# Accumulating transfers, early matmuls and a new inverse order in a gated mixer on one core

## The chip, the cores and the metric

The kernel runs on one core of one Trainium2 chip. The metric is the device time of one execution in microseconds (us), median of three. The core has a matrix engine (PE, whose weight loads are listed as PEld), a vector engine (DVE), a scalar engine (ACT), GpSimd (POOL) and a queue engine (SP). Each works through its own list of instructions in order; they meet through semaphores. Sixteen DMA engines serve the transfers that SP, ACT and POOL issue.

## The reference

All tensors are bf16 with 2048 rows and 640 columns, batch 1. The long convolution runs along the rows, one filter a column.

```python
def reference(A_q, A_k, A_v, A_shift_k, A_ssm_k, A_ssm_D, B_x, B_w1, B_w2, B_w3, B_w4, gate_w):
    x = A_q
    g = _sigmoid((x * gate_w).sum(-1, keepdims=True))
    a = _A_ref(x, A_k, A_v, A_shift_k, A_ssm_k, A_ssm_D)
    b = _B_ref(x, B_w1, B_w2, B_w3, B_w4)
    return g * a + (1 - g) * b

# _A_ref: a short and a long convolution
k_shift = sum over t in 0..3 of (k delayed by 3 - t rows) * shift_k[:, 3 - t]
kv = k_shift * v
y = causal convolution of kv with ssm_k (2048 taps a column, by FFT) + kv * ssm_D
return q * y

# _B_ref: a two-layer mixer
h = gelu(layernorm(x) @ w1)                    # 640 -> 640
hs = (the four column groups of h shifted by 1, -1, 2, -2 rows) @ w2
x1 = x + hs
return x1 + gelu(layernorm(x1) @ w3) @ w4      # 640 -> 1536 -> 640
```

## The kernel before, in words

Everything lives in one SBUF tensor, `arena`, 128 partitions wide, and one PSUM tensor, `PS`. A row t is held as block c (0 or 1), partition p and offset rho (0 to 7): t = 1024 c + 8 p + rho. So a "row tile" is one (c, rho), 128 x 640. PSUM is used as four pairs of banks; a job on PE takes a pair, and ACT empties it.

The mixer. For each rho, batch statistics on DVE (L756, L758) give mean and variance, POOL takes the inverse root as a power (L750), `normal` writes a normalized tile into one of four XN buffers (on DVE, L595), PE transposes it (L788), ACT evicts, the first product (L822) follows, ACT applies gelu (L621), and for the fifth column tile POOL issues small shifting transfers (L862, tag "tail"). The second product (L926) is added to x held in PSUM (L905); ACT evicts x1 with a row sum and squares it with another (L607). Four groups g of two rho each go through the second norm (`sum_group`, `normal`), a DMA transpose on SP (L945), the third product (L965, gelu on ACT) and the fourth (L983, after a seed of x1 that ACT writes into PSUM, L909).

The convolution. The taps are transposed (L729, evicted at L735). kv is built on DVE for each (c, h), four blocks: two multiplications of 5120 elements a partition into TA and TB (two taps each), their sum (5120), a sum of the halves (2560) and the product with v (2560). A transform of 2048 points is split into two column halves (half 0, 1) and two classes of frequencies (kap 0, 1): `forward` does its matrix part (L1014) for taps ("h") and kv ("k"). Then DVE runs four product units in the order (0,0), (0,1), (1,0), (1,1): `butterfly` on both, `window` on kv, `pointwise` (complex products) and `fold`. All units use slots s0 and s1 as temporaries. `inverse` (L1137) follows for half 0 after the second unit and for half 1 after the fourth: eight tiles of 8 matmuls, two ACT evictions each scaled by the gate, then on DVE a product with q and a sum into X (tag "fin"), and transfers out on SP (L1156).

The order on each engine is not that of the code. The class `Prog` records nodes with their reads, writes and an estimated cost, and `_forward` simulates the engines, taking next what can start first and, among equals, what the table `PRIO` puts higher (by tag and stage). Its result is the program's order. Waits follow from the recorded reads and writes. `add_dma`, a transfer on POOL that adds its source to its target, exists in the kernel before, but the lists `KV_DMA` and `PW_DMA` that choose it are empty. `WARM` is 40: a single job of matmuls on a tensor of ones at the start, whose result nobody reads.

Of the kernel before, what the change touches and what calls it, by code (L numbers as in the profile page):

```python
# [31 lines left out]
class Node:  # L32
    __slots__ = ("idx", "eng", "fns", "deps", "users", "cost", "bytes", "kind", "job", "prio", "first", "seed",
                 "start", "end", "base", "ordinal", "seq", "waits", "inc", "value", "sem", "final", "snap", "missing",
                 "tag", "soft")

    def __init__(self, idx, eng, fns, cost, kind, tag):
        self.idx = idx
        self.eng = eng
        self.fns = fns  # L40
        self.cost = cost
        self.kind = kind
        self.tag = tag
        self.deps = set()
        self.users = []
        self.bytes = 0
        self.job = None
# [12 lines left out]
        self.missing = 0  # L60
        self.soft = ()

# [24 lines left out]
class Prog:  # L87
# [69 lines left out]
    def pe(self, fns, r=(), cols=0, tag="", job=None, bits=(True, True)):  # L157
# [3 lines left out]
        node = self._new("pe", fns, cost, "c", r, (), None, tag)  # L161
        node.first = not job.nodes
# [6 lines left out]
    def dma(self, queue, fn, r=(), w=(), nbytes=0, cost=0.4, kind="dma", group=None, final=False, tag=""):  # L169
        node = self._new(queue, [fn], cost, kind, r, w, group, tag)  # L170
        node.bytes = nbytes
        node.final = final
        return node
# [18 lines left out]
    RATE = 405e3  # L192

    def _forward(self):
# [8 lines left out]
        free = {e: 0.0 for e in ENGS}  # L203
# [5 lines left out]
        link = 0.0  # L209
        xlink = 0.0  # L210
        alink = 0.0
        LAT = self.LAT
# [16 lines left out]
        while left:  # L229
# [41 lines left out]
            free[e] = t + n.cost  # L271
            if n.kind == "c":
                n.end = t + n.cost
            elif n.kind == "dma":
                link = max(link, t + 0.8) + n.bytes / self.RATE
                n.end = link + (1.1 if n.final else 1.7)
# [3 lines left out]
            else:  # L280
                xlink = max(xlink, t + 1.0) + 1.2
# [115 lines left out]
def _bf16_bits(a):  # L397
# [5 lines left out]
WARM = 40  # L403
KV_DMA = []
PW_DMA = []
# [3 lines left out]
INV = (0, 1, 2, 3, 4, 5, 6, 7)  # L409
SEED2 = []  # L410
SEED4 = (0, 1, 2, 3, 4, 5, 6, 7)
PRIO = {
# [67 lines left out]
def bass_gated_mix__ssm_conv_h3__mixer_s_mlp__prompt_kernel(  # L480
# [42 lines left out]
    oST = alloc(11 * 128)  # L523
# [38 lines left out]
    MV1, VAR1, RS1, MV2, S1, S2, MEAN2, TMP2, VAR2, RS2 = [stat(i) for i in range(10)]  # L562
# [17 lines left out]
    def c_ts(n):  # L580
        return 0.07 + n / 3700.0

    def c_act(n, aps=0, acc=False, psum=True):
        return (0.05 if psum else 0.09) + n * 0.000833 + 0.1 * aps + (0.16 if acc else 0.0)
# [92 lines left out]
    for c in range(5):  # L677
# [7 lines left out]
    P.pe([(lambda e, ps: e.matmul(bank(ps, 0, 128), ones, ones, start=True, stop=True)) for _ in range(WARM)], r=[ones],  # L685
         cols=128 * WARM * 2, tag="warmpe", bits=(False, None))
# [92 lines left out]
    def normal(rho, c, mean, rs):  # L779
# [15 lines left out]
    for rhos in LN1_GROUPS:  # L795
        P.stage = rhos[0]
        bn_group(MV1, VAR1, RS1, rhos)
        for rho in rhos:
# [35 lines left out]
    for sc in range(4):  # L834
# [10 lines left out]
        for j, d0 in enumerate(SHIFT):  # L845
# [4 lines left out]
            for carry, lst in todo.items():  # L850
# [9 lines left out]
                else:  # L860
                    i = i.rearrange("p (r q) -> p r q", r=n)
                P.dma("pool", lambda e, ps, o=o, i=i: e.dma_start(o, i), r=[i], w=[o], nbytes=32 * 512 * n,  # L862
                      cost=0.55, group="tail", tag="tail")
# [47 lines left out]
    for g in range(4):  # L911
# [27 lines left out]
        else:  # L939
            sum_group(rhos)  # L940
        for rho in rhos:
            for c in range(2):
                b = normal(rho, c, MV2[:, rho, 2 * c:2 * c + 1] if g in LN2_DVE else MEAN2[:, rho, c:c + 1], RS2)
# [182 lines left out]
    def inverse(half, slot0, slot1, Qh):  # L1126
        P.stage = half
        Qs = [cplx(s).rearrange("p (r i b) d -> p r i b d", r=4, i=2) for s in (slot0, slot1)]
        for rho in INV:
# [12 lines left out]
            gb = XN[gy_i[0] % 4]  # L1142
            gy_i[0] += 1
            for c in range(2):
# [3 lines left out]
            g2 = gb.rearrange("p (c d) -> p c d", c=2)  # L1148
            hs = slice(320 * half, 320 * half + 320)
            tt(g2, g2, Qh[:, :, rho, :], ALU.mult, 640, tag="fin")  # L1150
            tt(X[:, :, rho, hs], X[:, :, rho, hs], g2, ALU.add, 640, tag="fin")
            if rho % 2 == 1:
                for c in range(2):
                    src = X[:, c, rho - 1:rho + 1, hs]
                    dst = rows(out, c)[:, rho - 1:rho + 1, hs]
                    P.dma("sp", lambda e, ps, src=src, dst=dst: e.dma_start(dst, src), r=[src], nbytes=128 * 1280,  # L1156
                          final=True, tag="out")
# [48 lines left out]
```

## Time and profile before

| what | value |
|---|---|
| median of three runs | 243.61 us (243.39 to 244.1) |
| profiled execution, its own time | 244.46 us |
| its span, first to last instruction | 242.4 us |
| busy: PE, DVE, ACT, POOL | 224.5, 221.8, 157.4, 32.8 us |
| mean granted clock of PE | 0.970 |
| bytes moved by DMA | 27.67 MB |
| products of two tiles on DVE (L590) | 184, 194.3 us |
| one-tile scalings on DVE (L595) | 47, 14.7 us |
| scalings and squares on ACT from SBUF (L607) | 18, 12.4 us |

Times inside the profile count from the start of the span. L12 is line 12 of the kernel. The line of a helper stands for all that records through it: L590 is every two-operand operation on DVE, L595 every scaling there, L621 every ACT eviction, L633 every load. PE's busy time comes from modelled ends, so a stretch that is called busy can hold waiting; counts of matmuls in a window tell more. Of a group "a | b, c | d <- e" a is the shape and count, b the busy us, c the mean ns of one, d the idle us before it and e what ended it.

### The profile page before, as it was taken

What the parts mean: (1) busy time and instruction counts of PE and PEld (TensorE: products, weight loads), DVE (VectorE), ACT (ScalarE), POOL (GpSimd) and SP (SyncE); (2) the same over time, 40 slices, a digit from 0 to 9 for tenths busy, and PEclk for the clock granted to TensorE, in tenths of its full rate; (3) what the DMA queues carried; (4) which work ended last, traced back from release to release, by engine and by line L of the source; (5) the groups of instructions that cost most, each with busy time, mean ns of one, the idle gap of its engine ahead of it and who ended that gap; (6) DMA issues with size and microseconds to landing.
All of it is one profiled execution on the core that took longest, in us unless ns stands there. A gap on an engine that the chain in (4) does not pass through costs nothing.

```text
span 242.4 us, 3935 instructions
## 1 busy us (share of the span) xinstructions
PE 224.5 (93%) x1574; PEld 142.3 (59%) x1586; DVE 221.8 (92%) x290; ACT 157.4 (65%) x255; POOL 32.8 (14%) x38
## 2 busy tenths in 40 slices
PE   7279989999999999699999999999999999999991
PEld 6147654678754577454475655576444677577770
DVE  3998889999999899989999989789999999999484
ACT  2066685489999998968744668752554951564583
POOL 1323743340014002040005000000000000000000
PEclk9756999999999999999999999999999999999999
DMA  6999998010029910905000083200080541010055
GB/s 227 389 416 331 356 395 257 7 41 1 3 65 334 177 33 0 315 12 108 4 0 0 0 108 67 45 3 0 0 216 3 127 117 30 0 54 3 0 162 164
DMA packets 26483, 27.67 MB, mean 114 GB/s; under 512 B 12657, under 2 KB 22258, under 8 KB 26338
## 3 DMA queue, kind: packets, MB, share of 16 engines
q1 hardware_dynamic: 24674, 21.57, 31.3%
q0 software_dynamic: 1648, 5.54, 7.2%
q10 hardware_dynamic: 144, 0.33, 0.5%
q8 instruction: 12, 0.20, 0.4%
q14 instruction: 5, 0.04, 0.1%
HBM read 21.66 MB, written 2.62 MB: 100 GB/s over the span
## 4 chain that ended last, share of the span: by engine, by line
PE 66%; ACT 16%; DVE 11%; POOL 3%; DMA 2%; issue 1%; ACTq 0%; DVEq 0%
PE PS L983 22%; PE PS L965 21%; ACT arena L621 11%; PE PS L1137 7%; DVE arena L590 7%; PE PS L1014 6%; PE PS L926 4%; ACT arena L735 4%; POOL arena L750 3%; PE PS L822 2%; DVE arena L595 2%; DMA arena<-in_A_q_dram 2%; DVE arena L756 2%; PE PS L788 1%; ACT arena L607 1%
## 5 line engine op out<-in xcount | busy, mean ns | idle before, releaser
L590 DVE TENSOR_TENSOR arena<-arena 128x2560 bf16<-128x2560 bf16 (+4 forms) x184 | 194.3, 1110 | 8.6 <-ACT arena L621 6.6
L621 ACT ACTIVATE arena<-PS 128x640 bf16<-128x640 f32 (+3 forms) x132 | 97.7, 831 | 45.4 <-PE PS L965 20.7
L965 PE MATMUL PS<-arena 128*128 128x512 bf16 x232 | 51.7, 379 | 2.5 <-ACT arena L621 2.0
L983 PE MATMUL PS<-arena 128*128 128x320 bf16 x384 | 53.5, 299 | 0.0
L621 ACT ACTIVATE arena<-PS,arena 128x320 bf16<-128x320 f32 (+1 forms) x48 | 27.7, 622 | 33.2 <-PE PS L983 31.1
L983 PEld LDWEIGHTS PS<-arena 128*128 128x128 bf16 x384 | 37.5, 98 | 15.2 <-ACT PS L909 0.2
L965 PEld LDWEIGHTS PS<-arena 128*128 128x128 bf16 x240 | 23.3, 98 | 29.4 <-issue 2.4
L1014 PE MATMUL PS<-arena 128*128 128x320 bf16 x224 | 34.2, 300 | 0.7 <-ACT arena L621 0.5
L1014 PEld LDWEIGHTS PS<-arena 128*128 128x128 bf16 x224 | 19.5, 97 | 14.4 <-ACT arena L621 6.6
L822 PE MATMUL PS<-arena 128*128 128x512 bf16 (+1 forms) x121 | 24.7, 361 | 1.8 <-ACT arena L621 1.4
L926 PE MATMUL PS<-arena 128*128 128x320 bf16 x160 | 24.3, 299 | 0.0
L750 POOL TENSOR_TENSOR arena<-arena 128x4 f32<-128x4 f32 (+1 forms) x9 | 17.5, 1949 | 37.5 <-DVE arena L590 26.3
L822 PEld LDWEIGHTS PS<-arena 128*128 128x128 bf16 x125 | 12.8, 106 | 11.5 <-issue 1.7
L926 PEld LDWEIGHTS PS<-arena 128*128 128x128 bf16 x160 | 15.7, 98 | 6.1
L595 DVE TENSOR_SCALAR arena<-arena 128x640 bf16<-128x640 bf16 (+3 forms) x47 | 14.7, 355 | 4.3 <-POOL arena L750 3.3
L1137 PE MATMUL PS<-arena 128*128 128x320 bf16 x128 | 18.0, 299 | 0.0
L756 DVE BATCH_NORM_STATS2 arena<-arena 128x6 f32<-128x320 bf16 x32 | 13.4, 463 | 3.6 <-DMA arena<-in_A_q_dram 2.7
L1137 PEld LDWEIGHTS PS<-arena 128*128 128x128 bf16 x128 | 12.5, 98 | 5.2 <-issue 0.3
L788 PE MATMUL PS<-arena 128*128 128x128 bf16 x80 | 7.2, 253 | 6.3 <-DVE arena L595 6.3
L607 ACT ACTIVATE arena<-arena 128x640 bf16<-128x640 bf16 (+2 forms) x18 | 12.4, 694 | 0.2
L862 POOL DMA_DIRECT2D arena<-arena x18 | 9.7, 543 | 18.5 <-ACT arena L621 18.5
L909 ACT ACTIVATE PS<-arena 128x640 f32<-128x640 bf16 x16 | 11.0, 734 | 0.1
(33 smaller groups left out, 71.3 us busy)
## 6 DMA issues: line engine op xcount, KB each, us to landing
arena<-in_B_w_dram POOLq DMA_DIRECT2D x4, 960.0 KB, 7.9
arena<-in_A_v_dram SPq DMA_DIRECT2D x4, 640.0 KB, 12.1
arena<-in_A_k_dram SPq DMA_DIRECT2D x4, 640.0 KB, 11.3
arena<-in_A_ssm_k_dram SPq DMA_DIRECT2D x5, 512.0 KB, 19.0
arena<-in_A_q_dram SPq DMA_DIRECT2D x4, 640.0 KB, 4.8
out_dram<-arena SPq DMA_DIRECT2D x16, 160.0 KB, 2.0
arena<-in_A_q_dram SPq DMA_DIRECT2D x7, 320.0 KB, 7.2
arena<-cG POOLq DMA_DIRECT2D x1, 1024.0 KB, 5.2
```

Of the source, the lines that this page charges most:

```text
L590: return dve(lambda e: e.tensor_tensor(o, a, b, op), [a, b], [o], c_tt(n), tag=tag, **kw)
L595: return dve(lambda e: e.tensor_scalar(o, a, s1, s2, op0=op0, **kw2), [a] + sc, [o], c_ts(n), tag=tag, **kw)
L607: node = P.op("act", lambda e, ps: e.activation(o, i, func, **kw), r=r, w=[o], cost=c_act(n, naps, acc is not None, psum=False), tag=tag, ...
L621: node = P.op("act", lambda e, ps: e.activation(ov, inner(ps), func, **kw), r=r, w=[o], cost=c_act(n, len(r), acc is not None), job=job, t ...
L750: P.op("pool", lambda e, ps: e.tensor_tensor(r, v, hv, ALU.pow), r=[v, HALF], w=[r], cost=1.1, tag="ln")
L756: dve(lambda e, o=o, x=x: e.bn_stats(o, x), [x], [o], 0.393, tag="bn", group=("bn", id(mv), rho, c))
L822: fns.append(lambda e, ps, b=b, c=c, lhsT=lhsT: e.matmul(bank(ps, b, 256 * n), lhsT, XT[:, c, r0:r0 + n, :], start=(c == 0), stop=(c == 4)))
L926: fns.append(lambda e, ps, hh=hh, ft=ft, lhsT=lhsT: e.matmul(bank(ps, hh, 320), lhsT, w2v[:, ft, 320 * hh:320 * hh + 320], start=False, st ...
L965: fns.append(lambda e, ps, b=b, ft=ft, c=c, sc=sc: e.matmul(bank(ps, b, 512), w3v[:, c, 128 * ft:128 * ft + 128], XT[:, c, 2 * sc:2 * sc + ...
L983: fns.append(lambda e, ps, hh=hh, ft=ft, lhsT=lhsT: e.matmul(bank(ps, hh, 320), lhsT, w4v[:, ft, 320 * hh:320 * hh + 320], start=False, st ...
L1014: fns.append(lambda e, ps, w=w, b=b, rhs=rhs, st=(first and n == 0), en=(n == len(ss) - 1): e.matmul(bank(ps, b, 320), w, rhs, start=st, s ...
L1137: fns.append(lambda e, ps, kap=kap, ri=ri, c=c, r=r, s=s, n=n: e.matmul(bank(ps, c, 320), GM[:, kap, ri, r, s, :], Qs[kap][:, r, ri, c, :] ...
```

## The change

- `KV_DMA = [1]`: for block c = 1, both h, the sum of TA and TB (5120) is no longer a DVE instruction but two accumulating transfers on POOL, of half of the tile each.
- `PW_DMA = [1, 2]`: in the units (0,1) and (1,0) two of the ten operations of `pointwise` (2560 each) become an accumulating transfer each.
- The 40 matmuls on ones become 35 jobs of five, which the planner may put wherever PE is free.
- `LN1_ACT`, `LN2_ACT`: the normalization of rho 4 to 7 in the first norm and of groups 1 to 3 in the second moves from DVE to ACT (an Identity with scale and bias), and a small DVE product makes the bias.
- `INV = (0, 4, 2, 6, 1, 5, 3, 7)`: the order of the inverse's tiles. `FIN2 = (0,)`: in half 0 the closing product and sum take two tiles (rho and rho + 4) at once. Transfers out go by one rho with both blocks rather than by two rhos of one block; their number and size stay.
- The planner's estimates change (start times of the engines, transfer rates, a clock model for PE, costs of some operations), and `PRIO` is replaced, so the order of instructions changes on all engines.

```diff
-    RATE = 405e3
+    RATE = 400e3
+    WINDOW = 3.4133
+    PHASE = 2.4
...
-        free = {e: 0.0 for e in ENGS}
+        free = {"pe": 1.0, "act": 0.7, "dve": 0.8, "pool": 1.1, "sp": 0.7}
...
+            cost = n.cost
+            if n.array:
+                w = int((t - self.PHASE) // self.WINDOW)
+                while window < w:
+                    warm = duty > (0.42 if warm else 0.75) * self.WINDOW
+                    window += 1
+                    duty, carry = carry, 0.0
+                if not warm:
+                    cost += n.array
...
-                link = max(link, t + 0.8) + n.bytes / self.RATE
-                n.end = link + (1.1 if n.final else 1.7)
+                link = max(link, t + 1.2) + n.bytes / self.RATE
+                n.end = link + n.land
...
-                xlink = max(xlink, t + 1.0) + 1.2
+                xlink = max(xlink, t + 1.0, link) + 1.2
...
-WARM = 40
-KV_DMA = []
-PW_DMA = []
+FILL = 35
+KV_DMA = [1]
+PW_DMA = [1, 2]
...
-INV = (0, 1, 2, 3, 4, 5, 6, 7)
-SEED2 = []
+LN2_ACT = (1, 2, 3)
+LN1_ACT = [4, 5, 6, 7]
+INV = (0, 4, 2, 6, 1, 5, 3, 7)
+FIN2 = (0,)
+SEED2 = ()
...
     def c_ts(n):
-        return 0.07 + n / 3700.0
+        return 0.068 + n / 2220.0
...
-    P.pe([(lambda e, ps: e.matmul(bank(ps, 0, 128), ones, ones, start=True, stop=True)) for _ in range(WARM)], r=[ones],
-         cols=128 * WARM * 2, tag="warmpe", bits=(False, None))
+    for _ in range(FILL):
+        P.pe([(lambda e, ps: e.matmul(bank(ps, 0, 128), ones, ones, start=True, stop=True)) for _ in range(5)], r=[ones],
+             cols=128 * 5, tag="fill", bits=(False, None))
...
+    def minus(nb, mean, rs):
+        dve(lambda e: e.scalar_tensor_tensor(out=nb, in0=mean, scalar=-1.0, in1=rs, op0=ALU.mult, op1=ALU.mult),
+            [mean, rs], [nb], 0.15, tag="ln")
...
+        if nb is not None:
+            act(b, X[:, c, rho, :], ACTF.Identity, 640, scale=rs[:, rho, c:c + 1], bias=nb[:, rho, c:c + 1], tag="xn")
+            return b
...
-        bufs = [normal(rho, c, MV1[:, rho, 2 * c:2 * c + 1], RS1) for c in range(2)]
+        bufs = [normal(rho, c, MV1[:, rho, 2 * c:2 * c + 1], RS1, NB1 if rho in LN1_ACT else None) for c in range(2)]
...
+        if g in LN2_ACT:
+            minus(NB2[:, rsl, 0:2], mean[:, rsl, :], RS2[:, rsl, 0:2])
...
+            pair = rho // 4 == 1 and half in FIN2
+            if half in FIN2 and not pair:
+                continue
...
+            if pair:
+                g2 = V(oXN + 640 * (i - 1), 1280).rearrange("p (s c d) -> p c s d", s=2, c=2)
+                sel = slice(rho - 4, rho + 1, 4)
...
+            n = 1280 if pair else 640
+            tt(g2, g2, Qh[:, :, sel, :], ALU.mult, n, tag="fin")
+            tt(xs, xs, g2, ALU.add, n, tag="fin")
+            for r1 in range(sel.start, sel.stop, 4):
+                dst = out[0].rearrange("(c p r) d -> p c r d", c=2, r=8)[:, :, r1, hs]
+                src = X[:, :, r1, hs]
```

The transfer that the two lists choose is unchanged:

```python
def add_dma(o, i, nbytes, tag):
    return P.dma("pool", lambda e, ps: e.dma_start(o, i, accum_op=ALU.add, max_dma_last_dim=2560), r=[o, i], w=[o], nbytes=nbytes, cost=0.9,
                 kind="acc", tag=tag)
```

More of the change, by code (lines that the diff above doesn't have):

```diff
@@ L61, in __init__ @@
         self.soft = ()
+        self.array = 0.0
+        self.land = 2.2
 def _granules(ap):
@@ L167, in pe, with dma @@
         return job
-    def dma(self, queue, fn, r=(), w=(), nbytes=0, cost=0.4, kind="dma", group=None, final=False, tag=""):
+    def dma(self, queue, fn, r=(), w=(), nbytes=0, cost=0.4, kind="dma", group=None, final=False, tag="", land=None):
         node = self._new(queue, [fn], cost, kind, r, w, group, tag)
@@ L172, in dma @@
         node.final = final
+        node.land = land or (1.1 if final else 2.2)
         return node
@@ L211, in _forward @@
         alink = 0.0
+        warm = False
+        window = -1
+        duty = carry = 0.0
         LAT = self.LAT
@@ L270, in _forward @@
             n.start = t
-            free[e] = t + n.cost
+            cost = n.cost
[7 more added lines that the diff above has]
+                    cost += n.array
+                if n.tag != "shk":
+                    inside = min(cost, self.PHASE + (w + 1) * self.WINDOW - t)
+                    duty += inside
+                    carry += cost - inside
+            free[e] = t + cost
             if n.kind == "c":
-                n.end = t + n.cost
+                n.end = t + cost
             elif n.kind == "dma":
-                link = max(link, t + 0.8) + n.bytes / self.RATE
-                n.end = link + (1.1 if n.final else 1.7)
+                link = max(link, t + 1.2) + n.bytes / self.RATE
+                n.end = link + n.land
             elif n.kind == "acc":
@@ L560, in stat @@
         return V32(oST + f * 128, 64).rearrange("p (r i) -> p r i", r=8)
-    MV1, VAR1, RS1, MV2, S1, S2, MEAN2, TMP2, VAR2, RS2 = [stat(i) for i in range(10)]
+    MV1, VAR1, RS1, MV2, S1, S2, MEAN2, TMP2, VAR2, RS2, NB2, NB1 = [stat(i) for i in range(12)]
     def gcol(f):
@@ L1147, in inverse @@
                 evict(job, o, lambda ps, c=c: bank(ps, c, 320), ACTF.Copy, 320, scale=GG[:, gi:gi + 1], tag="gy")
-            g2 = gb.rearrange("p (c d) -> p c d", c=2)
+            pair = rho // 4 == 1 and half in FIN2
+            if half in FIN2 and not pair:
+                continue
             hs = slice(320 * half, 320 * half + 320)
[L1150 to L1157, printed above, removed]
+            if pair:
+                g2 = V(oXN + 640 * (i - 1), 1280).rearrange("p (s c d) -> p c s d", s=2, c=2)
+                sel = slice(rho - 4, rho + 1, 4)
+            else:
+                g2 = gb.rearrange("p (c s d) -> p c s d", c=2, s=1)
+                sel = slice(rho, rho + 1)
+            xs = X[:, :, sel, hs]
+            n = 1280 if pair else 640
[4 more added lines that the diff above has]
+                src = X[:, :, r1, hs]
+                P.dma("sp", lambda e, ps, src=src, dst=dst: e.dma_start(dst, src), r=[src], nbytes=128 * 1280,
+                      final=True, tag="out")
         P.stage = ""
```

21 lines of the change are left out of this document (14 added, 7 removed), and 45 rows, old and new, of the table PRIO.

## The prediction

> **What bounds the kernel now.** I read the page's summary first, then the chain in order of time, then the groups by form, the windows and the waits. The page (busy us, and 40 slices of 6.06 us each):
>
> ```profile
> span 242.4 us, 3935 instructions
> ...
> PE 224.5 (93%) x1574; PEld 142.3 (59%) x1586; DVE 221.8 (92%) x290; ACT 157.4 (65%) x255; POOL 32.8 (14%) x38
> ...
> PEclk9756999999999999999999999999999999999999
> ...
> PE 66%; ACT 16%; DVE 11%; POOL 3%; DMA 2%; issue 1%; ACTq 0%; DVEq 0%
> ```
>
> PE and DVE are both over 90% busy, and PE had about half its clock in slices 2 to 4. The windows show where PE's time goes to waste (columns: window, length, PE, PEld, DVE, ACT, POOL busy with counts, clock, DMA share, GB/s):
>
> ```profile
> 10.60:24.30 13.70, 12.14 (x78) 8.23 (x79) 12.28 (x44) 7.91 (x11) 4.14 (x8) 0.55 1.03 377
> 24.30:48.30 24.00, 22.60 (x220) 13.42 (x222) 22.16 (x19) 14.61 (x17) 10.72 (x10) 1.00 0.73 255
> 67.00:82.00 15.00, 14.39 (x96) 7.46 (x94) 14.86 (x18) 15.00 (x28) 3.55 (x4) 1.00 0.74 209
> 95.20:103.20 8.00, 6.00 (x45) 3.96 (x45) 8.00 (x8) 7.88 (x17) 1.75 (x2) 1.00 0.73 243
> ```
>
> The end of the chain (start, length, what) shows that PE runs into the last evictions without a break:
>
> ```profile
> 223.19 3.26 PE PS L983 x24
> 226.45 10.88 PE PS L1137 x80
> ...
> 237.42 0.53 ACT arena L621
> ...
> 238.92 0.49 DVE arena L590
> ```
>
> **PE's floor.** From stretches of the chain where matmuls follow each other at full clock: 320 columns take 0.136 us (24 in 3.26), 512 columns 0.2155 (10 in 2.16), 256 columns half of that, a transpose 0.0655 (40 in 2.62). The code issues 928 x 0.136 = 126.0, 315 x 0.2155 = 67.9, 50 x 0.1075 = 5.4, 160 transposes 10.5, the gate's 85 single columns 2.4, the tap broadcast's eight 1.1: 213.3 us, and none of it is touched. The first transpose starts at 10.6 and 5.1 us follow the last matmul (237.3 to 242.4). So PE loses 242.4 - 213.3 - 10.6 - 5.1 = 13.4 us in between: in 10.6 to 24.3 it does 40 transposes, 30 matmuls of 256 columns and the eight (6.95 us of work in 13.7: 6.75 lost); 24.3 to 48.3 about 1.2; 67 to 82 does 92 x 0.136 = 12.5 in 15.0 (2.5 lost; ACT is 15.00 busy, evicting 640 columns in 0.6 us for each 0.54 us of matmuls); 95.2 to 103.2 45 x 0.136 = 6.1 in 8.0 (1.9, ACT again); 1.05 elsewhere.
>
> **The DVE chain.** From 83 us until the last fold at 223.8 (209.24 + 14.56 in DVE's timeline) DVE has hardly a gap: the four product units follow each other because they share two temporaries. Its prices by form:
>
> ```profile
> L590 DVE TENSOR_TENSOR arena<-arena 128x2560 bf16<-128x2560 bf16 x70 | 100.5, 1483 | 0.3
> ...
> L590 DVE TENSOR_TENSOR arena<-arena 128x5120 bf16<-128x5120 bf16 x12 | 33.7, 2821 | 0.1
> ...
> L595 DVE TENSOR_SCALAR arena<-arena 128x640 bf16<-128x640 bf16 x32 | 12.4, 437 | 4.3 <-POOL arena L750 3.3 <-DMA arena<-arena 0.9
> L607 ACT ACTIVATE arena<-arena 128x640 bf16<-128x640 bf16 x16 | 12.0, 753 | 0.2
> ```
>
> **The change, part by part.** *Off DVE:* two kv additions of 5120 (2 x 2.82 = 5.64), four product sums of 2560 (4 x 1.483 = 5.93), 8 first and 12 second normalizations (20 x 0.437 = 8.74); the first half's final products go in pairs (16 x 0.489 = 7.82 becomes 8 x 0.818 = 6.54, saving 1.28); five bias products come in (0.2 each by the 0.23 row, 1.0). Sum: 20.6 us less.
>
> *On to ACT:* 20 x 0.753 = 15.1 us by the square's row, the nearest. Eight lie near 27 to 38, where ACT is 3.9 to 4.7 busy of each 6: free. Twelve (9 us) belong to the second norm; transposes on SP and the third product wait for ACT now instead of DVE. ACT is full from 54 to 102 (46.6 of 48 us), and after that idle for 2 us and more at a time between evictions, so they cost 0 (late) to 9 (early); I take 1, set off below.
>
> *The adds:* eight of 640 KB issued on POOL, 0.87 each (the weight loads there took 0.85 to 0.88). No row shows one. The nearest by size, the q loads of 640 KB, landed in 4.8; the v loads in the crowded start in 12.1. A small transfer between arena ranges landed in 1.8 when nothing else ran, so 4.8 is 1.8 plus 3.0 for bytes. An add also reads its target: I take half again, 4.5. In a unit the second add goes out two products (2.97) after the first and two more products cover it: it lands at 0.87 + 1.8 + 2 x 4.5 = 11.7, the products end at 5.9, DVE stalls 5.8. With 1 for kv, whose fourth-block products can run meanwhile: 2 x 5.8 + 1 = 12.6. Ends: 3.0 for bytes gives 2.7 a unit (6 in all, less if a window step fills in, so even nothing); the 12.1 row gives 10.3 for bytes, 17.3 a unit, 36 in all. Queued behind an add on POOL: the powers of the second norm and the w3, w4 and table loads, hence the third product; each waits at most for the products ahead of the add, and DVE's slack holds that.
>
> So the last fold ends at 223.8 - 20.6 + 12.6 = 215.8. After it PE needs 64 x 0.136 = 8.7 and the 5.1 of the end: a span of 229.6 by this chain, under PE's own figure below, so the stalls cost nothing. They decide beyond a sum of 16.4.
>
> *Early matmuls:* 175 in fives instead of 40. Forty took 4.45 us; 175 take 11.5 (0.0655 each) to 18.7 (0.107), so from 1.06 they reach past 10.6 and, in the gaps, beyond. A started five holds a real matmul up for 0.33 to 0.54, at most some eight times: 0 to 4, on PE time that waits for DVE anyway; I take 0. If the clock stays full, 6.95 us of work in 10.6 to 24.3 takes 6.95. But it helps only if DVE delivers: there it is 12.3 of 13.7 busy with the statistics, and 24 to 38 alternates kv products with normalizations behind a power of 3.5 us on POOL. Eight of those moving to ACT, the work up to the last of the first product (6.95 + 22.8 = 29.8) could end at 40.4 instead of 48.3. Of 7.95 lost I take back 6.5 (bounds: -4 and 7.95).
>
> *The rest:* the forward stretches keep the 0.6 against 0.54, but second-layer products, sooner ready, can lie between: 2.5 of 4.4 back, less 1 for ACT, net 1.5 (bounds -9, 4.4). Head: the first variance step stood 0.36 behind statistics of the next row, and the first transposes waited for both blocks: 0.5 (0 to 1.5). The last fold frees four of eight inverse tiles before its last two steps: today PE has other work until 226.45, 2.65 after the fold, so 0. Elsewhere 0.5 of 1.05. The output transfers keep count and size; the queue on SP gains none.
>
> Sum: 6.5 + 1.5 + 0.5 + 0.5 = 9.0. The profiled execution took 244.46 for its span of 242.4, 0.85 over the median of 243.61. It becomes 235.5 (span 233.4 = 10.1 + 213.3 + 4.9 lost + 5.1); from the median, **234.6**.
>
> **Rivals.**
> *ACT takes over.* If the twelve fall into 54 to 102, PE waits for evictions some 6 us more: 240.6. For: ACT 15.00 of 15. Against: in 108 to 150, where most of them lie now, ACT idles before evictions. 0.13.
>
> *Adds at half the rate.* Reading two operands where a load reads one would double the byte part to 6.0: 8.7 a unit, 18.5 in all, fold at 221.7, span 235.5: 236.7. The row is the 4.8 us load, and nothing here shows an add. The Trainium skill, "Collectives: The Full Stack", Part 3, says the adding transfer runs at half the copy's rate because it reads two sources; no run here shows that yet. 0.10.
>
> *DVE starves POOL's issue.* A power on POOL took 3.53 beside a 2.82 product and 0.71 to 1.04 without: if adds wait like that, 2.5 each, some 5 a unit and 2.5 for kv, 25.1 in all, fold at 228.3, span 242.1: 243.3. Against: four POOL transfers issued at 49.7 to 51.3 landed in 1.8 to 2.0 beside products without a gap. The Trainium skill, "SBUF — State Buffer", "SBUF: two separate sides", warns that a DMA from that queue stands while DVE holds the shared port; its later section excepts two-input products, as the 1.8 does. 0.04.
>
> *Nothing gained.* The clock drops again after the fills, or fills delay the transposes as much as they speed them: 243.5. 0.05.
>
> *Slower: the adds' bytes.* If one needs 9.6 us for its bytes (68 GB/s; the q load did 218), each middle unit stalls 16: 33 in all, fold at 236.2, span 250.0: 251.2. It is slower than now from a sum of 26, which is 7.9 us (83 GB/s) an add. For: the 12.1 row, and that no such transfer is in the trace. Against: from 100 us on the queues are nearly empty. 0.13.
>
> **Numbers.** Forecast 0.55, own range 228.5 (all 13.4 and 1.5 of the head back: 228.7) to 239. A measurement here tells 0.3%, 0.73 us, apart. Faster: 0.55 + 0.10 + 0.12 of ACT's 0.13 = 0.77. Within: 0.04 + 0.05 = 0.09. Slower: 0.13 + 0.01 = 0.14. The range 228.5 to 244.5 leaves out the slow case and little else.
>
> **What would show it.** Right: clock full from the second slice on, DVE near 201 busy, ACT near 172, the first product's last matmul before 43, DVE gaps of 3 to 9 ahead of the two subtractions of the middle units, PE unbroken to the last inverse. Wrong: a chain ending in DVE and DMA, gaps over 12 there, or PE waiting for ACT between 54 and 102.

## The result, and the profile after

The changed kernel takes 254.52 us (median of four runs, 250.85 to 256.79) against 243.50 us of the kernel before on the same chip (243.34 to 244.10): a ratio of 1.0365, 95% interval 1.0245 to 1.0485. It is slower by 9 to 11 us; forecast was 234.6, some 9 us faster. The ratio leaves out the two longest of the four runs, the profiled one among them, and so lies below the quotient of the medians (1.045); differences between this kernel and its variants are therefore given by medians and by ratios, and read from the traces as well. The profiled execution took 254.89 us for a span of 253.1.

The page after, in the lines that answer to those of before:

```profile
span 253.1 us, 4195 instructions
...
PE 233.6 (92%) x1711; PEld 149.2 (59%) x1721; DVE 202.8 (80%) x261; ACT 171.7 (68%) x275; POOL 38.6 (15%) x46
...
PEclk9999998999999999899999999999999999999899
...
DVE 45%; ACT 17%; DMA 15%; PE 9%; SPq 8%; issue 3%; POOL 1%; ACTq 0%; DVEq 0%; POOLq 0%
```

The early matmuls did hold the clock up, DVE did lose 19 us of work and ACT did gain 14. But the chain, which was 66% PE, is now 45% DVE and 15% DMA, with 9% PE. The chain in order of time (start, length, what) shows where:

```profile
21.96 14.46 DMA arena<-in_gate_w_dram
...
36.74 3.87 PE PS L859 x10
...
90.79 6.30 ACT arena L647 x12
...
98.08 1.57 DVE arena L616 x2
...
145.07 8.88 DMA arena<-arena
...
184.71 11.99 DMA arena<-arena
...
218.06 19.86 DVE arena L616 x16
...
238.06 10.54 PE PS L1178 x64
```

Four things are to be seen. The load of the gate's weights, issued behind all but one of the kv loads, lands 14.5 us later; PE, which stood 4.0 us for it, then runs ten matmuls of 512 in 3.87 us instead of 2.16, at a granted clock of 0.59 from 36.47 to 40.60. The first window step (98.08) starts when ACT has evicted the part of the kv transform that it reads (half 0, class 0); before, it started at 83.10. Two of the chain's pieces are accumulating transfers, the second sums of the two middle units (L655). And PE's last 64 matmuls start at 238.06, only when the third of the last fold's six steps has ended (237.91; the fold ends at 240.12). They take 10.54 us where 64 x 0.136 = 8.7 were counted: PE had stood for 3.6 us, and the granted clock was 0.52 from 238.06 to 241.50. (The Trainium skill, "TensorE: Matmul & The Clock Gate", Part 1, puts the idle time after which the clock falls at one window of some 3.4 us. The waits of 4.0 and 3.6 us agree; but the clock also fell after two waits of 2.8 us, to 0.64 from 106.01 to 109.50 here and to 0.53 in f_xn2 below, and it stood at 1.00 after one of 3.2 us in a_noadd. The length of a wait alone does not decide here.)

The windows (columns as in the prediction) show PE's front:

```profile
10.60:24.30 13.70, 13.65 (x147) 10.24 (x146) 12.39 (x43) 10.94 (x16) 7.26 (x12) 1.00 1.04 354
24.30:48.30 24.00, 19.07 (x118) 9.82 (x119) 19.70 (x13) 16.13 (x21) 6.13 (x6) 0.93 0.79 270
```

The clock column rose from 0.55 to 1.00 in the first, but in the second PE did 118 matmuls instead of 220. The waits of DVE (what it waited for: us in total, times, longest):

```profile
DVE arena L621 <- ACT arena L647: 13.5, 3, 6.7
DVE arena L616 <- DMA arena<-arena: 8.9, 2, 6.3
DVE arena L616 <- issue: 5.4, 1, 5.4
DVE arena L616 <- ACT arena L647: 5.4, 3, 3.5
```

The first row belongs to the front, the two between to the middle units. Of the last row 3.5 us are the wait ahead of the first window step, 1.0 comes at 180.05 and 1.0 behind the last fold. The lines of DVE's timeline for the window step, the first from the kernel before, and for the middle units (start, length, line, shape, count, idle before and what ended it):

```profile
83.10 7.55 DVE L590 TENSOR_TENSOR arena<-arena 128x1280 bf16<-128x1280 bf16 x8 [0.59 <-ACT arena L621]
...
98.08 20.24 DVE L616 TENSOR_TENSOR arena<-arena 128x1280 bf16<-128x1280 bf16 x18 [3.47 <-ACT arena L647]
...
154.03 25.02 DVE L616 TENSOR_TENSOR arena<-arena 128x2560 bf16<-128x2560 bf16 x24 [6.33 <-DMA arena<-arena]
...
191.25 2.96 DVE L616 TENSOR_TENSOR arena<-arena 128x1280 bf16<-128x1280 bf16 x3 [5.44 <-issue]
196.78 45.34 DVE L616 TENSOR_TENSOR arena<-arena 128x2560 bf16<-128x2560 bf16 x45 [2.56 <-DMA arena<-arena]
```

The time up to the last fold can be split at the first window step, with the gaps that DVE's timeline marks added up on both sides:

| | before | after |
|---|---|---|
| first window step starts | 83.10 | 98.08 |
| DVE idle ahead of it | 7.4 | 30.1 |
| from there to the end of the last fold | 140.7 | 142.0 |
| of that DVE idle | 4.5 | 15.3 |
| last fold ends | 223.80 | 240.12 |
| from there to the end of the span | 18.6 | 13.0 |

So DVE's work fell by 7.7 us ahead of the window step (83.10 - 7.4 against 98.08 - 30.1) and by 9.5 behind it (136.2 against 126.7). Ahead of it the saving became waiting and the step came 15 us later; behind it the waits ate the saving.

### The profile page after: what moved, and what is told of

Its sections match the earlier page's. It is cut to its first block, busy times and chain, and to the rows that moved or that the text cites. A ratio compares the mean times of both kernels' runs of the same rounds, so it can differ in the third digit from the quotient of the medians.

```text
span 253.1 us, 4195 instructions
## 1 busy us (share of the span) xinstructions
PE 233.6 (92%) x1711; PEld 149.2 (59%) x1721; DVE 202.8 (80%) x261; ACT 171.7 (68%) x275; POOL 38.6 (15%) x46
## 3 DMA queue, kind: packets, MB, share of 16 engines
q0 software_dynamic: 5360, 10.78, 20.6%
## 4 chain that ended last, share of the span: by engine, by line
DVE 45%; ACT 17%; DMA 15%; PE 9%; SPq 8%; issue 3%; POOL 1%; ACTq 0%; DVEq 0%; POOLq 0%
DVE arena L616 45%; ACT arena L647 11%; DMA arena<-arena 10%; SPq L659 8%; DMA arena<-in_gate_w_dram 6%; PE PS L1178 4%; PE PS L859 4%; ACT arena L762 4%; ACT arena L633 2%; POOL arena L899 1%; PE PS L963 1%; POOL arena L655 0%; PE PS L822 0%; PE PS L942 0%; ACTq L1227 0%
## 5 line engine op out<-in xcount | busy, mean ns | idle before, releaser
L616 DVE TENSOR_TENSOR arena<-arena 128x1280 bf16<-128x1280 bf16 (+5 forms) x170 | 181.6, 1126 | 25.3 <-DMA arena<-arena 8.9
L1006 PE MATMUL PS<-arena 128*128 128x512 bf16 x233 | 53.0, 385 | 3.2 <-ACT arena L633 2.8
L1024 PE MATMUL PS<-arena 128*128 128x320 bf16 x384 | 53.3, 299 | 0.0
L1024 PEld LDWEIGHTS PS<-arena 128*128 128x128 bf16 x384 | 37.5, 98 | 15.0 <-ACT PS L946 0.2
L1006 PEld LDWEIGHTS PS<-arena 128*128 128x128 bf16 x240 | 23.6, 99 | 30.9 <-issue 4.7
L1055 PE MATMUL PS<-arena 128*128 128x320 bf16 x224 | 34.7, 300 | 1.1 <-ACT arena L647 0.6
L633 ACT ACTIVATE arena<-arena 128x640 bf16<-128x640 bf16 (+2 forms) x38 | 30.3, 832 | 1.7 <-DVE arena L807 1.5
L1055 PEld LDWEIGHTS PS<-arena 128*128 128x128 bf16 x224 | 19.7, 98 | 15.1 <-ACT arena L647 7.4
L963 PE MATMUL PS<-arena 128*128 128x320 bf16 x160 | 24.3, 299 | 0.0
L1178 PE MATMUL PS<-arena 128*128 128x320 bf16 x128 | 19.7, 316 | 3.6 <-DVE arena L616 3.6
L655 POOL DMA_DIRECT2D arena<-arena x8 | 10.5, 1424 | 71.7 <-DVE arena L616 71.0
L621 DVE TENSOR_SCALAR arena<-arena 128x640 bf16<-128x640 bf16 (+3 forms) x27 | 6.9, 289 | 17.8 <-ACT arena L647 13.5
L777 POOL TENSOR_TENSOR arena<-arena 128x4 f32<-128x4 f32 (+1 forms) x9 | 13.8, 1531 | 41.5 <-DVE arena L616 29.2
L963 PEld LDWEIGHTS PS<-arena 128*128 128x128 bf16 x160 | 15.7, 98 | 6.1
L1178 PEld LDWEIGHTS PS<-arena 128*128 128x128 bf16 x128 | 13.1, 103 | 10.0 <-issue 4.2
L859 PEld LDWEIGHTS PS<-arena 128*128 128x128 bf16 x125 | 12.2, 101 | 11.1 <-issue 1.9
L783 DVE BATCH_NORM_STATS2 arena<-arena 128x6 f32<-128x320 bf16 x32 | 13.5, 463 | 2.6 <-DMA arena<-in_A_q_dram 2.6
L712 PE MATMUL PS<-arena 128*128 128x128 bf16 x175 | 12.7, 245 | 1.1 <-DVE arena L669 1.1
L712 PEld LDWEIGHTS PS<-arena 128*128 128x128 bf16 x175 | 12.2, 112 | 1.6 <-DVE arena L669 1.1
## 6 DMA issues: line engine op xcount, KB each, us to landing
arena<-in_A_ssm_k_dram SPq DMA_DIRECT2D x5, 512.0 KB, 11.7
```

What stands on the lines that cost most here:

```text
L616: return dve(lambda e: e.tensor_tensor(o, a, b, op), [a, b], [o], c_tt(n), tag=tag, **kw)
L633: node = P.op("act", lambda e, ps: e.activation(o, i, func, **kw), r=r, w=[o], cost=c_act(n, naps, acc is not None, psum=False), tag=tag, ...
L777: P.op("pool", lambda e, ps: e.tensor_tensor(r, v, hv, ALU.pow), r=[v, HALF], w=[r], cost=1.1, tag="ln")
L859: fns.append(lambda e, ps, b=b, c=c, lhsT=lhsT: e.matmul(bank(ps, b, 256 * n), lhsT, XT[:, c, r0:r0 + n, :], start=(c == 0), stop=(c == 4)))
L963: fns.append(lambda e, ps, hh=hh, ft=ft, lhsT=lhsT: e.matmul(bank(ps, hh, 320), lhsT, w2v[:, ft, 320 * hh:320 * hh + 320], start=False, st ...
L1006: fns.append(lambda e, ps, b=b, ft=ft, c=c, sc=sc: e.matmul(bank(ps, b, 512), w3v[:, c, 128 * ft:128 * ft + 128], XT[:, c, 2 * sc:2 * sc + ...
```

## The experiments

In all of these kernels but the last two, the order of every engine is written out, not planned: it is that of the kernel named as the base, with the moves that are told. They run on several chips, so each is compared with the kernel before on its own chip (243.96, 244.30, 244.28 and 244.44 us). A helper's line number differs from kernel to kernel: L723, L724 and L754 below are the same two-operand DVE operations as L616. Medians from two chips can differ by up to 0.9 us for that reason alone (243.50 against 244.44 for the kernel before); the ratios do not have this.

**One part at a time, on the kernel before.** First the kv sums (b_kva), with the third block's transfers behind the tail's on POOL and the fourth's behind a table load (one power moves up with them, ahead of a weight load):

```diff
-KV_DMA = []
+KV_DMA = [1]
```

> The kernel before in its own order, with only the two kv sums of block c = 1 made by four accumulating transfers. Theory A (kv's transfers cost because the next block's products write the same two temporaries): the next block's first product waits until both transfers have landed, some 9 us after the last product, where the sum took 2.8; twice, so the last kv step ends 10 to 14 us later, the first window step too, and the time is 253 to 258. Rival B (the transfers are hidden, ACT's 15 us of extra work made the change slower): 241 to 245. Rival C (the late loads of k and of the gate's weights made it slower): 241 to 245.

Measured: 263.69 us, ratio 1.081 (1.078 to 1.085). DVE's timeline (start, length, line, shape, count, idle before):

```profile
67.86 4.69 DVE L724 TENSOR_TENSOR arena<-arena 128x5120 bf16<-128x5120 bf16 x4 [8.59 <-DMA arena<-arena]
...
90.67 3.09 DVE L724 TENSOR_TENSOR arena<-arena 128x2560 bf16<-128x2560 bf16 x2 [13.31 <-DMA arena<-arena]
```

Both column halves of a block use the same TA and TB. So the fourth block's first product (67.86) waits 8.6 us until the third block's sums have landed, and the sum of its own halves (90.67) waits another 13.3 for its own transfers: 21.9 us of waiting for 5.6 us of work taken off. The prediction let the fourth block's products run meanwhile.

The same with temporaries of its own for the fourth block (b_kvabuf), in XT (the transposed rows of the first norm), its products right behind the third's, and its transfers ahead of the table load:

```diff
-    for c in range(2):
-        TA = V(oTAP if c == 0 else oS, 5120)
-        for h in range(2):
+    kv_block(1, 0, V(oS, 5120), TB)
...
+    kv_block(1, 1, V(oXT, 5120), V(oXT + 5120, 5120))
```

> As the one before, but the fourth block's products go to two temporaries of their own (in the then unused area of the transposed tiles), right behind the third block's, and its two transfers are issued right behind the first two. Theory A: the products no longer wait; what is left is the four transfers' own length, one behind the other at 4.4 us each, so kv ends 2 to 5 us later than in the kernel before: 244 to 249. If the buffers are not the reason: as the run before, 253 or more. Rivals B and C: 241 to 245 for both.

Measured: 246.59 us, 1.0103 (1.0075 to 1.0132). The waits shrink to 5.09 and 2.77, and 17 of the 20 us are gone. The price of the transfers is thus mostly that of the shared temporaries and of the order that they force; but even with free ones four transfers in a row land at 63.8, 68.2, 71.2 and 74.4, later than DVE would have needed for the sums.

The product sums of the middle units alone (b_pwa):

```diff
-PW_DMA = []
+PW_DMA = [1, 2]
```

> The kernel before in its own order, with only the two product sums in each of the two middle units made by transfers. Theory A2 (the units are one chain on DVE, and each pair of transfers lands about 6 to 8 us after the last product that covers it, where the sums took 3.0): the first of the two units has 1.8 us of normalizations in between, the second nothing; net 2 and 4 us later at the last fold: 246 to 251. Rival (the stalls lie in DVE's slack under PE): 242 to 244.5. Rival B: 243 to 244.

Measured: 248.25 us, 1.0162 (1.0118 to 1.0205). DVE's timeline:

```profile
141.87 2.89 DVE L723 TENSOR_TENSOR arena<-arena 128x2560 bf16<-128x2560 bf16 x2 [5.26 <-DMA arena<-arena]
...
181.05 10.30 DVE L723 TENSOR_TENSOR arena<-arena 128x2560 bf16<-128x2560 bf16 x11 [6.65 <-DMA arena<-arena]
```

The sums stall DVE by 5.26 and 6.65 us (5.8 was the prediction's figure), and the loss is 4.3 us: the four sums of 1.48 us that left DVE do not pay for it, and the kernel before had only 2.65 us between its last fold and the matmuls that need it.

The early matmuls alone (b_fill), 35 jobs of five in the places that they have in the changed kernel:

```diff
-WARM = 40
+FILL = 35
```

> The kernel before in its own order, with only the 40 matmuls on ones at the start replaced by 35 fives, placed as in the changed kernel. By the prediction's step (PE at full clock from 10.6 us on takes back up to 6.5 us): 237 to 241. Theory D (until 38 us the loads and DVE set the pace, so a faster PE only waits more): 242.5 to 244, with the clock full in the second to fourth slice.

Measured: 242.87 us, 0.9954 (0.9934 to 0.9975, ten runs). The mean clock rises from 0.970 to 0.993. The second window:

```profile
24.30:48.30 24.00, 21.34 (x195) 11.69 (x198) 22.10 (x21) 12.54 (x14) 9.74 (x9) 0.93 0.74 258
```

The last matmuls of the first product still start at 47.99 (47.65 before), and the window step stands at 83.49 (83.10). So the higher clock shortens nothing in the front: there PE gets its work from DVE, which is 22.1 of 24 us busy. The gain is 1.1 us, not 6.5. The kernel before shows the same by itself: in its 17 runs on the last chip the mean granted clock lay between 0.959 and 1.000; the five at 0.998 or more took 244.36 to 244.80 us, the other twelve 244.11 to 244.79.

The second norm of groups 1 to 3 on ACT on top of that (f_xn2), twelve scalings and their bias products:

```diff
+LN2_ACT = (1, 2, 3)
```

> The kernel before in its own order with the early matmuls, and the second norm's scalings of groups 1 to 3 on ACT instead of DVE, put where ACT is free. DVE loses 5.2 us and gains 0.6 between 108 and 150. If DVE's chain of units bounded that kernel: 238 to 240. If PE, busy without a gap from 103 on, bounds it: 241.5 to 244, as with the early matmuls alone. Rival B (ACT's extra work delays evictions): 245 or more.

Measured: 246.61 us, 1.0101 (1.0057 to 1.0144), 3.7 us more than with the early matmuls alone. In PE's timeline the third product now waits until ACT has emptied a pair of banks of the fourth product (131.29 to 132.06), which ACT's list has behind four scalings (128.02 to 131.38):

```profile
132.12 4.02 PE L1116 MATMUL PS<-arena 128*128 128x512 bf16 x10 [2.77 <-ACT arena L761]
```

Ten matmuls take 4.02 us after that wait, almost twice their price at full clock; the granted clock was 0.53 from 132.12 to 135.50. In this order ACT's extra work is not free.

**Repairs of the changed kernel.** The product sums back on DVE, all else as changed (a_nopwa):

```diff
-PW_DMA = [1, 2]
+PW_DMA = []
```

> The changed kernel in its own order, with only the four product sums of the middle units back on DVE. Theory A2 (the pairs stall the DVE chain by 6.3 and some 8 us and save 5.9): 245 to 249. If the stalls lay in slack, or if the chain is bound elsewhere: 253 to 256.

Measured: 246.59 us, 1.0107 (1.0081 to 1.0133), 7.9 us less than the changed kernel by the medians, 6.3 by the ratios (0.0258 of 244). The first window step hardly moves (97.04), and from there to the end of the last fold it now takes 134.9 us instead of 142.0: 7.1 us of the gain are in the product units. The page:

```profile
PE 231.4 (95%) x1721; PEld 148.7 (61%) x1721; DVE 208.4 (85%) x265; ACT 172.0 (70%) x275; POOL 33.1 (14%) x42
...
PE 64%; ACT 17%; DMA 8%; SPq 8%; issue 1%; DVE 0%; ACTq 0%
```

With 5.6 us more work on DVE, DVE has left the chain.

The loads on SP in the order of their use, the gate's weights and kv's inputs ahead (a_load; the list is abbreviated):

```diff
 SP: x, kh1, w1, ...
-FM, shk, k3, x3, k0, kh0, k2, w2, v0, v2, v3, k1, gw, v1, ssm
+shk, x3, gw, k0, kh0, k1, v0, k2, v1, k3, v2, w2, v3, ssm, FM
```

> The changed kernel in its own order, with only the loads on SP in another order: the gate's weights and the first k and v blocks go ahead of w2, the later k and v blocks and the transform table. Theory C (work that was freed in the first 38 us only waits for loads: DVE 3.3 us for k at 36.2, PE 4.0 us for the gate's weights at 36.4, then 1.7 us at half clock): both waits go, the first product ends 4 to 6 us earlier, and as the order behind it is the same, the time falls to 248 to 251. Theory A alone (kv's transfers decide when the units start): 252 to 255.

Measured: 250.04 us, 1.024 (1.0195 to 1.0285), 4.5 us less by the medians, 3.1 by the ratios, whose intervals overlap. The second kv block starts at 31.9 instead of 36.2, and all that follows moves with it: the window step to 93.6, the last fold to 236.2. The stalls in the middle units stay (6.3 and 8.3).

Temporaries of its own for the fourth kv block (a_buf; the edit of b_kvabuf in the changed kernel):

> The changed kernel in its own order, with only the fourth kv block's products in temporaries of their own, right behind the third's. By theory A the DVE waits of 6.7 us before and some 9 us after these products shrink and kv ends some 8 to 12 us earlier (at 76 to 80 instead of 88.3). But PE and ACT keep the order in which the transform of kv comes behind most of the second product, and ACT is full from 57 to 98: so the units start at 92 to 97 instead of 98.1, and the time is 249 to 254. If kv's end alone set the start of the units: 242 to 246.

Measured: 252.25 us, 1.0337 (1.0275 to 1.04). The kv products end at 77.5 instead of 88.3, yet the window step comes only 1.4 us earlier (96.72), and its wait names ACT. The wait that costs most in b_kva is covered here by ACT's evictions.

Load order and product sums repaired together (a_mix):

> The changed kernel with two things at once: the loads issued in the order of their use, and the four product sums of the middle units back on DVE; the kv sums of the second block stay transfers. Theory (two separate costs, one in the front and one in the middle units): alone they gave 4.5 and 7.9 us, so together 12.4, from 254.5 to 242.1, with the first window step near 94 us and the last fold near 228. Rival (one chain: once DVE no longer waits for the sums, PE and ACT set the end, and the earlier front is not used): it stays within 1.5 us of the 246.6 that the sums alone gave, and PE waits for ACT instead.

Measured: 244.81 us, 1.0003 (0.9977 to 1.0028), the kernel before's time. It lies between the sum of both gains (242.1) and no addition (246.6): the load order still gives 1.8 us (2.5 by the ratios).

As a_mix, with the kv sums on DVE too, so that no accumulating transfer is left (a_noadd); DVE takes the last two kv blocks earlier in its list, ahead of the second norm's first sums:

```diff
-KV_DMA = [1]
-PW_DMA = [1, 2]
+KV_DMA = []
+PW_DMA = []
```

> As the kernel with both repairs, and the kv sums of the second block on DVE again as well: no accumulating transfer is left, while early matmuls, normalizations on ACT, the inverse's order and the closing pairs stay. Theory (the kv sums as transfers cost their wait of 6 to 13 us only where nothing else holds DVE; in this order ACT's stretch of evictions from 57 to 98 us holds the first window step anyway): no faster than the kernel with the kv transfers, 242 to 245, the kv products end some 6 us earlier and the window step moves by less than 2. Rival (the kv transfers set the front): 3 us or more faster than it, below 239.5.

Measured: 245.25 us, 1.0008 (0.9979 to 1.0038). The kv sums as transfers, 20 us in the order of the kernel before, cost nothing here. DVE's timeline of a_noadd:

```profile
80.61 0.17 DVE L759 TENSOR_SCALAR arena<-arena 128x4 f32<-128x4 f32 x1 [7.40 <-ACT arena L785]
...
93.73 6.08 DVE L754 TENSOR_TENSOR arena<-arena 128x1280 bf16<-128x1280 bf16 x6 [3.71 <-ACT arena L785]
```

DVE is through with kv at 69.9 instead of 83.9 and then waits for ACT; the window step is at 93.73 (93.71 in a_mix). ACT is 43.9 of 44 us busy between 54 and 98.

Is it that late window step which keeps this kernel from the forecast? In a_sk (a_noadd as the base) the kv transform of half 0 goes ahead on PE and ACT, and on DVE the window step goes ahead of the second norm's sums of group 1:

```diff
 ACT: ... taps' transform of half 0 (both classes)
+kv transform of half 0: eight evictions of class 0, four of class 1
 three squares, x1 of group 2 (called column tile 2 below), ...
-kv transform of half 0
```

> The changed kernel with loads in order of use and without any accumulating transfer, and with the kv transform of half 0 moved ahead: PE's products and ACT's evictions for both classes that the first window step needs come right behind the taps' transform, before the second products of column tile 2 and three squares; on DVE the butterflies and the window step go ahead of the second norm's sums of group 1. Theory (ACT, busy 44 of 44 us between 54 and 98, sets the window step by what it has in front of it): the window step starts at 88 to 90 instead of 93.7, but the evictions that are put off come due later, and the time stays at 244 to 246. Rival (the late window step is what keeps this kernel from the forecast): each us earlier is a us less, 240 to 241.

Measured: 244.27 us, 0.9993 (0.9984 to 1.0002). The window step comes 3.7 us earlier (90.00), the last fold ends at 229.87 (229.55 in a_noadd). The head start is spent on new waits in the next six us, 2.26 for ACT and 1.15 for POOL. So an earlier window step alone gains nothing here.

And the eight scalings of the first norm back on DVE, again in a_noadd (a_ln1):

```diff
-LN1_ACT = [4, 5, 6, 7]
+LN1_ACT = []
```

> The same kernel without accumulating transfers and with loads in order of use, but with the eight normalizations of the first norm (rho 4 to 7) on DVE again, as in the kernel before, and the transform's order as it was. Theory (DVE is late with kv there, ACT has room before 48): the kv products and the window step come 3.5 to 4 us later (8 x 0.437), 97 us, and the time rises by 3 to 4 to 248 to 249. Rival (ACT's evictions behind these eight set the window step): the window step does not move or comes earlier, and the time falls by up to 3.

Measured: 247.98 us, 1.0153 (1.0121 to 1.0184). The kv products end 3.1 us later, so does the window step (96.85), and the last fold ends 2.5 us later (232.05). Of the change's parts this is one that gains, 2.7 us by the medians and 3.5 by the ratios.

**Planned anew without transfers.** The changed code with neither transfers nor scalings on ACT, priorities chosen for it by the kernel's own estimates (with 2.4 us instead of 1.1 for POOL's power and 375 instead of 400 GB/s for transfers) (g_plain):

> The changed kernel's code without any accumulating transfer and without normalizations on ACT, but with early matmuls, the inverse's order and the closing pairs, and with priorities for the planner chosen anew for that. By the same estimates the kernel before plans to 240.4 and measures 243.6, this one to 237.3. Theory (the parts of the change that touch neither a transfer nor ACT gain, if the order fits them): 240.5, at most 242. Rival (the plan's gain is below what its estimates can tell): within 1 us of the 242.9 of the early matmuls alone, or slower.

Measured: 243.44 us, 0.9958 (0.9928 to 0.9988): early matmuls, closing pairs and inverse order gain no more than the early matmuls did alone.

The same with the second norm's twelve scalings on ACT (g_ln2):

> As the one before it, but with the second norm's 12 normalizations on ACT as in the changed kernel, and priorities chosen for that; planned to 237.7. Theory (ACT's extra work costs only where the order puts it ahead of evictions that PE waits for): 240.9, as good as without. Rival (ACT has no room in any order): 3 us slower than the one without, as those twelve cost 3.7 us in the order of the kernel before.

Measured: 242.66 us, 0.9931 (0.9905 to 0.9957), the fastest of all by its ratio, if only by 0.7%; its interval overlaps those of b_fill and g_plain. The page:

```profile
span 240.5 us, 4201 instructions
...
PE 230.5 (96%) x1711; PEld 147.9 (61%) x1721; DVE 216.5 (90%) x273; ACT 165.2 (69%) x267; POOL 30.4 (13%) x38
```

Its window step starts late too, at 95.1, but from there to the last fold it needs 132.4 us. Twelve scalings that cost 3.7 us in one order cost nothing in another.

## Why the prediction was wrong

*The counts were right.* DVE 202.8 (near 201), ACT 171.7 (near 172), a clock of 9 or more from the second slice on but for three slices at 8.

*The step that failed: "So the last fold ends at 223.8 - 20.6 + 12.6 = 215.8".* It took all work off one unbroken DVE chain. The prediction had itself found that chain only "From 83 us"; the kv sums, eight first scalings and part of the rest lie ahead of it. By the table of the result 7.7 us lie ahead, so that its sum puts the window step at 83.1 - 7.7 + 1 = 76.4 and needs 139.4 from there. Measured: 98.1 and 142.0. Of the 24.3 us by which the fold missed, 21.7 arose in the front and 2.6 in the product units. The fold at 240.1 and the 13.0 us behind it make the span of 253.1, where PE's own account was to set 233.4.

*The front.* In the kernel before ACT's last eviction of the kv transform of half 0, class 0, ends at 83.06 and the window step, which reads it, starts at 83.10: ACT released it, not DVE, which had waited 0.59 us. In that order work taken off DVE ahead of it could hardly bring it forward; no run takes off only such work. The prediction read "ACT 15.00 of 15" in that very stretch and used it for PE alone. In the changed kernel ACT released the step again, 15 us later. Two causes of that are measured: the load order that came with the new priorities, 4.4 us (a_load), which the change part by part does not mention, and the place of those evictions in ACT's list, which also came with the priorities. From 48 us to the window step ACT is busy for 33.4 of 35.1 us in the kernel before and for 42.2 of 45.7 us in a_mix. Ahead of the step its list there has 13 pieces more (x1 and squares of group 1, three x1 of group 2, two evictions of class 1), 9.1 us together. So of the 10.6 us by which a_mix still has its window step later than before, 8.8 are more work of ACT, and 1.8 are waits that were not separated. To put six of the 13 behind the step moved it 3.7 us, but gained no time (a_sk).

*"1 for kv, whose fourth-block products can run meanwhile"*: mis-sized. They share TA and TB; in the order of before the waits were 21.9 us (b_kva). In the changed kernel they cost nothing (a_mix against a_noadd), because DVE stood for ACT in the same places: the third block's sum landed at 62.6 and ACT let go at 63.2, the fourth's at 84.2 and 84.9. The two long ones of the three waits in the row of 13.5 us above (6.7 and 6.2) are these, so the row names ACT where two causes end together.

*The middle units, 2 x 5.8.* Right in size: 6.33 in the first, 5.26 and 6.65 in b_pwa; from the first issue to the second landing, 11.7 in the prediction, it took 11.7, 11.5 and 12.0. The parts of that sum were not right, so the agreement is in part luck: the first add was to land after 7.2 and the second 4.5 later; in b_pwa it was 5.9 and 5.7, and then 5.6 and 6.2 with other transfers beside the second. The second unit of the changed kernel stalled 8.0, because its transfers ran beside the q loads: a q load that takes 6.6 us in a_nopwa took 11.4, and the sum behind it 12.0. 5.4 of the 8.0 (the row that ends in issue) is DVE's closing product standing for that load, which landed at 191.18; it starts at 191.25. What failed is "the stalls cost nothing", since "They decide beyond a sum of 16.4" was reckoned from a fold at 215.8. With the fold on the chain they cost what DVE loses by them, 6 to 8 us.

*"Of 7.95 lost I take back 6.5".* The clock came to 1.00 and 0.93 in the two windows, and 1.1 us came of it (b_fill); the kernel before gains nothing in those of its runs that have the full clock. The caveat in the text, "it helps only if DVE delivers", was the answer. With the first scalings on ACT and the loads in order, the first product does end at 44.3 instead of 48.7 (a_mix), but that reaches no further than ACT's full stretch. PE's account, drawn up as in the prediction (length less matmuls at their price, without those on ones; some records are missing, so to about 1 us), shows the same: from 10.6 to 48.3 PE loses 8.4 us in the kernel before and 6.9 in a_noadd, where no accumulating transfer is left. From 95 to 104 it loses 1.0 more than before, standing 3.2 us for the third product's weights. The forecast mark, before 43, was missed: 49.2 in the changed kernel, for the gate's load. The small terms (1.5 for the forward stretches, 0.5 each for the head and elsewhere) can't be told apart behind this; g_plain, which has the new head, pairs and inverse order, shows nothing beyond the early matmuls.

*ACT, "I take 1".* 3.7 us in the order of before (f_xn2), nothing measurable in an order planned for it (g_ln2 against g_plain), a gain of 2.7 for the first norm's eight (a_ln1). The bounds 0 and 9 held; an order decides.

*The rivals.* The slower one came near the time (251.2) with the wrong mechanism: its 9.6 us of bytes for each transfer are nowhere in the traces. That the adds run at half the rate of a copy ("Collectives: The Full Stack", Part 3, of the Trainium skill, which says it of the adds in a collective) would be 6.0 us for the bytes. Queued kv sums land 3.0 to 4.8 apart here, so they are faster than that, and 4.5 was a fair choice for them. The second sums of the product units, whose target lies in rows of 640 bytes, land 4.1 to 8.6 after the first, but always beside other transfers: for them it stays open. DVE starving POOL's issue did not happen: the issues took 1.3 and 1.7 us beside DVE products without a gap (from 53.53) and 1.2 and 1.7 while DVE mostly stood (from 73.73), in keeping with the exception for two-input products that the prediction names from "SBUF — State Buffer" of the Trainium skill. "ACT takes over" was right in naming ACT and the stretch from 54 to 102, but saw PE, not DVE, wait for it.

## What to carry to other kernels

Before work taken off an engine is subtracted from a due time, the profile must be asked what released the first instruction of that chain: savings ahead of it count only if that engine itself was the last. A transfer that replaces an instruction needs free temporaries for the work that is to cover it, so the buffers that the next block shares come into the sum before the transfer's bytes do. A wait that the profile puts down to one engine can hide a second one that ends half a microsecond earlier; take both away before either is priced.

## What the runs showed of the hardware

The accumulating transfers by the issue row (count, KB each, median us from issue to landing):

```profile
arena<-arena POOLq DMA_DIRECT2D x8, 640.0 KB, 8.6
```

The issue on POOL takes 1.2 to 1.7 us (a weight load there took 0.87). A sum that meets no other transfer lands after 5.7 to 5.9 us, a kv sum that was issued 0.7 to 0.8 us behind another lands 3.2 to 4.8 after it, so the two that replace one DVE instruction of 2.82 us need 9 to 12 us. Beside each other a q load of 640 KB and a sum both slow down, to 11.4 and 12.0 us (the q load in a_nopwa: 6.6). Nearly all loads on SP land in the order of their issue: the gate's weights, issued at 21.96, came at 36.42, 0.2 us after the k load ahead of them; issued at 5.6 (a_load), they came at 15.3.
